# Talking-heads attention with a gated feed-forward: packing the last queries of three images, and another order inside a step

## The chip, the cores and the metric

The kernel runs on one core of a Trainium2 chip. The metric is the device time of one execution in microseconds (us); lower is better. TensorE (PE) multiplies matrices, VectorE (DVE) and ScalarE (ACT) work element by element and empty PSUM, where the products arrive, GpSimd (POOL) works on SBUF, SyncE (SP) mostly issues DMAs. In a profile PEld is the loading of weights into TensorE.

## The reference, cut to what matters

```python
def _attn_ref(q, k, v, w_pre, w_post):        # q, k, v: 4 images, 12 heads, 448 positions, 64
    scores = scale * np.matmul(q, k.transpose(0, 1, 3, 2))
    scores = np.einsum('bhij,hg->bgij', scores, w_pre)        # first mixing, over heads
    scores = scores - np.max(scores, axis=-1, keepdims=True)
    attn = np.exp(scores)
    attn = attn / (np.sum(attn, axis=-1, keepdims=True) + 1e-09)
    attn = np.einsum('bhij,hg->bgij', attn, w_post)           # second mixing
    return np.matmul(attn, v)

# then, with x = the attention's output as 1792 rows of 768:
#   xn = x / rms(x) * rms_g;  out = (silu(xn @ w_gate) * (xn @ w_val)) @ w_out
```

## The kernel before

**Chunks and steps.** An image's 448 query positions are cut into four chunks of 120, 120, 110 and 98 (`CHUNK`, `OFF`, `WIDE`); ten positions of the last one are computed with the third. The 16 chunks are numbered n; n % 4 == 3 is the last chunk of an image. A chunk is worked on in six steps (five in a last chunk), 92 steps t in all (`steps`, line 402), each on two groups u of 2 x 5 positions by all 12 heads.

**What a step does** (the loop at lines 494 to 554). The product of q and k is made well ahead: `qk_mm` (line 134) computes one pair of heads of a later chunk as four 64 x 64 products into two PSUM tiles `qk`, one per head j; `qk_evac` (line 152) copies them out to `st`, j = 0 on ACT (line 162), j = 1 on DVE (line 160), and issues one or two DMAs that scatter `st` to `r`, so that a row of `r` holds one head and one position. `premix` (line 181) multiplies `r` by `wk_pre`, which gives the first mixing `sp` for u = 0 and u = 1. DVE takes the negated row maxima `nm` (`rowmax`, line 196), ACT the exponential `e` with its sums (`expo`, line 203). `norm` (line 206) adds 1e-9 (`t`), takes the reciprocal (`rp`) on DVE and multiplies the second mixing's weights by it on POOL (`wn`, line 215). One step later `postmix` (line 217) multiplies `e` by `wn`, which gives the second mixing `pm`, transposed; `evac_a` (line 241) copies its two halves to `at_all`, on ACT (line 265) and DVE (line 263). `av_mm` (line 274) multiplies `at_all` with v, `av_copy` (line 296) copies the result out to `xt` on ACT, and POOL adds squares for the norm of x (`x_sum`).

**What sets the order.** The order on each engine is the order in which the loop's body is written; a scheduler moves nothing. Within a step the order on TensorE is

```python
                order = sp[:1] + qk[1:] + sp[1:] + qk[:1]     # line 511
```

that is: `sp` for u = 0, `qk` of head j = 1, `sp` for u = 1, `qk` of head j = 0; then `postmix` of the step before, then `av_mm`. The `qk` and `sp` tiles have one buffer per head and per u, so a product into one waits for the copy (or the exponential) that empties it. On DVE a step is: `nm`, `nm`, copy of `st`, copy of `at_all`, `t`, `rp`.

**Work beside it.** From step 23 on the first feed-forward weights are converted from float64 in pieces (`first_w`, line 774): eight rounds of seven steps, five of which have one DVE instruction on `wac` (`to_f32`, line 559). Scales of x, of the weights and of the gains are computed in chains of very small DVE instructions on `stats` and `square` (`chain`, line 443), and `sq_all` (line 349) the norm of x of one image, with four products of TensorE at its stage 0. The chains stand in `last_at`, at the end of a step.

**After step 91** come the feed-forward products, until the end.

The first five `qk` pairs of chunk 1 are made before the loop (`AHEAD`), and from then on one pair is made per step until all are done, at step 84.

## Time and profile before

| | us |
|---|---|
| three runs | 823.37, 830.76, 831.68 (median 830.76) |
| the profiled execution | 822.48 |
| its span, first to last instruction | 820.6 |
| PE busy / DVE busy / ACT busy | 794.4 (97%) / 634.5 (77%) / 507.3 (62%) |
| the 92 steps, from the first `nm` on | 317.75 |

The profile is of one execution. "Busy" counts the time in which an instruction ran; a busy TensorE is not one at its peak. Step t begins here with its first `nm` on DVE (two per step, one in the last step of an image), so that a stretch of the trace can be told by the number of `nm` in it. In rows of instructions the columns are start and duration in us, engine, line, operation, out<-in, and how many were merged; in brackets the engine's idle time before it and what ended it.

### The profile page before, as it was taken

The numbers are of one execution on the slowest core, as the hardware profiler recorded it, in microseconds if no ns is written. First come the engines' busy times: TensorE is split into PE (matmuls) and PEld (weight loads), VectorE is DVE, ScalarE is ACT, GpSimd is POOL, SyncE is SP. The second block draws the span as 40 slices with busy tenths as digits, with TensorE's granted clock in tenths as the row PEclk, the third lists the DMA queues.
The fourth block names the chain that finished last, engine by engine and source line by source line (L and its number), as shares of the span: only waits on it lengthen the run. The fifth ranks groups of instructions, "written<-read, shape, count | busy, mean of one in ns | idle before, by whom it ended". The sixth has DMA issues, their size and how long they took to land.

```text
span 820.6 us, 26914 instructions
## 1 busy us (share of the span) xinstructions
PE 794.4 (97%) x10806; PEld 485.2 (59%) x10806; DVE 634.5 (77%) x1322; ACT 507.3 (62%) x1133; POOL 350.4 (43%) x467
## 2 busy tenths in 40 slices
PE   7899999999999989899999999999999999999998
PEld 2567777767776767655555555555555555555555
DVE  5777878888798867888788978997889676547562
ACT  3677778777776867664344454545444546969850
POOL 7212343454355435843624433426144359452310
PEclk9999999999999999999999999999999999999999
DMA  7777777777876754564255644754546446566641
GB/s 216 208 216 217 219 229 222 228 219 232 222 234 200 211 147 150 158 230 118 66 177 150 183 129 127 216 149 121 174 145 201 133 127 184 157 199 176 184 135 67
DMA packets 81902, 145.15 MB, mean 177 GB/s; under 512 B 10527, under 2 KB 72797, under 8 KB 81779
## 3 DMA queue, kind: packets, MB, share of 16 engines
q1 hardware_dynamic: 79982, 139.83, 57.0%
q0 software_dynamic: 832, 2.06, 1.0%
q8 instruction: 85, 1.39, 0.7%
q10 hardware_dynamic: 965, 1.56, 0.6%
q14 instruction: 38, 0.31, 0.1%
HBM read 72.83 MB, written 31.88 MB: 128 GB/s over the span
## 4 chain that ended last, share of the span: by engine, by line
PE 86%; DMA 8%; DVE 2%; issue 1%; ACT 1%; POOL 1%; SPq 0%; ACTq 0%; DVEq 0%; POOLq 0%
PE qk L140 7%; PE pm L226 7%; PE sp L187 7%; PE av L294 6%; PE pg L750 6%; PE pg L752 6%; PE pv L752 6%; PE pg L751 6%; PE pv L751 6%; PE pv L750 6%; DMA r<-st 6%; PE po L751 6%; PE po L750 6%; PE po L752 6%; DMA wraw<-in_wgv 1%
## 5 line engine op out<-in xcount | busy, mean ns | idle before, releaser
L187 PE MATMUL sp<-r,wk_pre 64*64 64x448 f32 x720 | 167.4, 542 | 5.4 <-DMA r<-st 3.5
L203 ACT ACTIVATE e<-sp,nm 128x448 f32<-128x448 f32 x180 | 114.3, 637 | 84.8 <-DVE nm L196 82.4
L140 PE MATMUL qk<-k,q 64*64 64x448 f32 x768 | 152.6, 559 | 5.9 <-DMA q<-in_q 4.1
L196 DVE TENSOR_REDUCE nm<-sp 128x1 f32<-128x448 f32 x180 | 110.3, 620 | 44.1 <-PE sp L187 27.4
L215 POOL TENSOR_SCALAR wn<-wk,rp 128x60 f32<-128x60 f32 x180 | 59.5, 345 | 181.8 <-DVE rp L212 109.7
L226 PEld LDWEIGHTS pm<-wn,e 60*64 60x64 f32 x5040 | 106.1, 134 | 37.6 <-POOL wn L215 23.8
L226 PE MATMUL pm<-wn,e 60*64 60x60 f32 x5040 | 106.7, 220 | 4.2 <-issue 4.1
L798 POOL TENSOR_TENSOR sg<-sg,u 128x448 f32<-128x448 f32 x36 | 45.9, 1275 | 151.2 <-ACT sg L795 106.7
L294 PE MATMUL av<-at_all,v 64*64 64x240 f32 (+6 forms) x1728 | 93.6, 316 | 4.6 <-issue 2.6
L750 PE MATMUL pv<-x,wh 128*128 128x448 f16 x264 | 93.0, 352 | 0.0
L752 PE MATMUL pv<-x,wl 128*128 128x448 f16 x264 | 93.0, 352 | 0.0
L752 PE MATMUL pg<-x,wl 128*128 128x448 f16 x264 | 93.0, 352 | 0.0
L751 PE MATMUL pv<-x,wh 128*128 128x448 f16 x264 | 93.0, 352 | 0.0
L751 PE MATMUL pg<-x,wh 128*128 128x448 f16 x264 | 93.0, 352 | 0.0
L750 PE MATMUL pg<-x,wh 128*128 128x448 f16 x264 | 93.0, 352 | 0.0
L750 PE MATMUL po<-h,fac 128*128 128x448 f16 (+1 forms) x258 | 89.8, 348 | 0.0
L751 PE MATMUL po<-h,fac 128*128 128x448 f16 (+1 forms) x258 | 89.8, 348 | 0.0
L752 PE MATMUL po<-h,fac 128*128 128x448 f16 (+1 forms) x258 | 89.8, 348 | 0.0
L750 PEld LDWEIGHTS <-wh 128*128 128x128 f16 x528 | 51.7, 98 | 48.2 <-issue 0.2
L751 PEld LDWEIGHTS <-wh 128*128 128x128 f16 x528 | 51.7, 98 | 48.3 <-issue 0.3
L752 PEld LDWEIGHTS <-wl 128*128 128x128 f16 x528 | 51.7, 98 | 48.2
L187 PEld LDWEIGHTS sp<-r,wk_pre 64*64 64x64 f32 x720 | 60.3, 133 | 27.2 <-ACT e L203 13.2
(167 smaller groups left out, 1567.3 us busy)
## 6 DMA issues: line engine op xcount, KB each, us to landing
r<-st SPq DMA_DIRECT2D x117, 210.0 KB
hraw<-td SPq DMA_DIRECT2D x84, 224.0 KB
wraw<-in_wgv SPq DMA_DIRECT2D x20, 768.0 KB
td<-keep SPq DMA_DIRECT2D x48, 224.0 KB
wraw<-in_wo SPq DMA_DIRECT2D x12, 768.0 KB
r<-st SPq DMA_DIRECT2D x44, 157.5 KB
v<-in_v SPq DMA_DIRECT2D x24, 256.0 KB
k<-in_k SPq DMA_DIRECT2D x24, 224.0 KB
```

Of the source, the lines that this page charges most:

```text
L140: nc.tensor.matmul(ps[j][m, :S], qt[n][sl, hp, m], kt[n // NC, hp][sl], start=True, stop=True)
L187: nc.tensor.matmul(o, wk_pre[sl], rt[n][sl, 2 * p + v_], start=True, stop=True)
L196: nc.vector.tensor_reduce(t, ps[:, :S], AX.X, ALU.max, negate=True)
L203: nc.scalar.activation(e, ps[:, :S], AF.Exp, bias=nmx.pop((n, p, u)), accum_out=sm[n, p][:, u : u + 1])
L215: nc.gpsimd.tensor_scalar(wn[n, p][:, u], wk, r[:, u : u + 1], 1.0, ALU.mult, ALU.mult)
L226: nc.tensor.matmul(o[:, :, at_], e_[sl, j : j + JT], w_[sl].rearrange("p (s i) -> p s i", s=2), start=True, stop=True)
L294: nc.tensor.matmul(x, vt[b, hp][sl, j, c_], a, start=(c_ == 0), stop=(c_ == JC - 1))
L750: nc.tensor.matmul(ps, a, xh[:, kk, at_], start=(kk == 0), stop=False)
L751: nc.tensor.matmul(ps, a, xl_[:, kk, at_], start=False, stop=False)
L752: nc.tensor.matmul(ps, a2, xh[:, kk, at_], start=False, stop=(kk == KT - 1))
L798: nc.gpsimd.tensor_tensor(h, sg, u, ALU.mult)
```

## The change

For images two to four (`shared(n)` is true for the last chunk of each) the last chunk no longer has a score tile of 128 columns of q. Of its positions 24 are computed in the eight columns that each of the other three chunks leaves free, and the other 64 as a half tile: `qk_mm` then makes two pairs of heads at once, so that the chunk needs three steps with `qk` instead of six. The scores of positions that travel with another chunk are scattered by additional DMAs (`rest_out`) into a new tile `rest`, from which the first and the last step of that chunk take their first mixing, with a second arrangement of weights in `wk_pre`. The steps with `qk` are no longer one per step in a row: those of chunk n begin one step after chunk n - 2 has begun (`starts`), so four steps in the middle and all from step 80 on have none.

Inside a step `av_mm` now comes ahead of `postmix`, and `norm` ahead of the copies of `at_all` and of POOL's sums. The conversion of weights and the small chains are moved from the ends of a step to the place between `rowmax` and the copy of `st` (`odd_at`), the chains one step later than they stood; `sq_all` and the scales of x begin at other steps. `st` is one tile for twelve heads instead of twelve buffers. The scratch space for descriptors of POOL's DMAs is halved.

```diff
+def shared(n):
+    return n >= NC and n % NC == NC - 1
...
+        def two(j, i):
+            sl, u = slice(64 * j, 64 * j + 64), (i + j) % 2
+            nc.tensor.matmul(ps[i][64 * u : 64 * u + 64, :S], qt[n][sl, 2 * hp + i], kt[n // NC, 2 * hp + i][sl], start=True, stop=True)
+
+        if shared(n):
+            return [[lambda j=j, i=i: two(j, i) for j in (i, 1 - i)] for i in range(2)]
...
+        if j and n >= NC and hp % 3 == 2:
+            rest_out(n, hp // 3, st)
+        if shared(n):
+            for u in range(2):
+                waiting.append((n, 2 * (2 * hp + j) + (u + j) % 2, st[64 * u : 64 * u + 64, at_], 0, SPLIT, False))
+            if at_ < 3 or at_ == 5:
+                for args in waiting:
+                    gather(*args)
+                waiting.clear()
...
+    def rest_out(n, half, st):
+        if shared(n):
+            for i in range(2):
+                for u in range(2):
+                    rows = slice(100 + 12 * u, 112 + 12 * u)
+                    nc.sync.dma_start(rest[rows, slot(n - 3 + i)], st[64 * u + 60 + 2 * i : 64 * u + 62 + 2 * i, :6])
+        else:
+            nc.sync.dma_start(rest[4 + half : 4 + half + 95 : 2, slot(n)], st[120:, 6 * half : 6 * half + 6])
...
+        last = shared(n)
+        kind = int(last and p in (0, PAIRS[-1] - 1))
+
+        def rows(sl, i):
+            if not kind:
+                return rt[n][sl, i - 2 * last]
+            return rest[sl, slot(n - 3 + (i if p == 0 else 2))]
...
-            nc.tensor.matmul(o, wk_pre[sl], rt[n][sl, 2 * p + v_], start=True, stop=True)
+            nc.tensor.matmul(o, wk_pre[sl, kind], rows(sl, 2 * p + v_), start=True, stop=True)
...
-    for i, a in enumerate([(n, hp) for n in range(1, NCHUNK) for hp in range(H // 2)][AHEAD:]):
-        qk_at[i].append(a)
+    odd_at = [[] for _ in range(T + 40)]
+    starts, t_ = {}, -1
+    for n in range(1, NCHUNK):
+        for hp in range(H // 4 if shared(n) else H // 2):
+            if n == 1 and hp < AHEAD:
+                continue
+            t_ = max(t_ + 1, first[n - 2] + 1 if n > 1 else 0)
+            starts.setdefault(n, t_)
+            qk_at[t_].append((n, hp))
...
-                job(first[n] + i, lambda i: first_w(i), i)
+                (odd_at if i % 7 < 5 else jobs_at)[first[n] + i].append((lambda i: first_w(i), i))
...
-        t = first[NC * b + NC + 2] + (5 if b < B - 2 else 3)
-        for i in range(17):
-            last_at[t + max(i - 2, 0) // 3].append((sq_all, b, i))
-        chain(t, lambda b=b: x_scale_ops(b), 2 if b < B - 2 else 4)
+        t = (first[10] - 1, first[13] + 4, first[14] + 3)[b]
+        for i in range(16):
+            last_at[t + (max(i - 1, 0) if i < 4 else 3 + (i - 4) // 3)].append((sq_all, b, i))
+        chain((first[6] + 8, first[10] + 6, first[14] + 3)[b], lambda b=b: x_scale_ops(b), 1 if b < B - 2 else 2)
...
                 rowmax(*back(0))
-                flush()
+                flush(1)
+                for f, *a in odd_at[t]:
+                    f(*a)
                 expo(*back(0))
             if t in (T - 2, T):
                 early(t - T)
+            for a in av_at[t]:
+                av_mm(*a)
             if back(1):
                 postmix(*back(1))
-            for a in av_at[t]:
-                av_mm(*a)
             for a in qk_at[t][:1]:
                 for j in range(2):
                     qk_evac(*a, j)
-            if back(0) and t >= T - 2:
+            if back(0):
                 norm(*back(0))
+            flush()
             if back(1):
                 for v_ in range(2):
                     evac_a(*back(1), v_)
...
+            for x in last_at[t]:
+                f, *a = x
+                if t >= T - 1 or f is sq_all and not a[1]:
+                    f(*a)
+                else:
+                    odd_at[t + 1].append(x)
```

How this moves instructions is seen at three places. First VectorE before, steps 31 and 32, in the second round of the weights' conversion (`nm` are the row maxima, `wac` the conversion's tile):

```order
L565 TENSOR_SCALAR wac<-wac 128x384
L196 TENSOR_REDUCE nm<-sp 128x1 x2
L160 COPY st<-qk 128x448
L263 COPY at_all<-pm 128x84x5
L210 TENSOR_SCALAR t<-s 128x2
L212 RECIPROCAL rp<-t 128x2
L566 TENSOR_SCALAR wac<-wac 128x384
L196 TENSOR_REDUCE nm<-sp 128x1 x2
L160 COPY st<-qk 128x448
L263 COPY at_all<-pm 128x84x5
L210 TENSOR_SCALAR t<-s 128x2
L212 RECIPROCAL rp<-t 128x2
```

and VectorE now, the same two steps:

```order
L241 TENSOR_REDUCE nm<-sp 128x1 x2
L617 TENSOR_SCALAR wac<-wac 128x384
L194 COPY st<-qk 128x448
L255 TENSOR_SCALAR t<-s 128x2
L257 RECIPROCAL rp<-t 128x2
L308 COPY at_all<-pm 128x84x5
L241 TENSOR_REDUCE nm<-sp 128x1 x2
L618 TENSOR_SCALAR wac<-wac 128x384
L194 COPY st<-qk 128x448
L255 TENSOR_SCALAR t<-s 128x2
L257 RECIPROCAL rp<-t 128x2
L308 COPY at_all<-pm 128x84x5
```

The instruction on `wac` stood ahead of a step's maxima and now stands between them and the copy of `st`; `t` and `rp` stood behind the copy of `at_all` and now stand ahead of it.

Second VectorE before, steps 34 and 35:

```order
L568 SCALAR_TENSOR_TENSOR wac<-wraw,wac 128x384
L196 TENSOR_REDUCE nm<-sp 128x1 x2
L160 COPY st<-qk 128x448
L263 COPY at_all<-pm 128x84x5
L210 TENSOR_SCALAR t<-s 128x2
L212 RECIPROCAL rp<-t 128x2
L196 TENSOR_REDUCE nm<-sp 128x1 x2
L160 COPY st<-qk 128x448
L263 COPY at_all<-pm 128x84x5
L210 TENSOR_SCALAR t<-s 128x2
L212 RECIPROCAL rp<-t 128x2
```

and VectorE now, the same two steps:

```order
L241 TENSOR_REDUCE nm<-sp 128x1 x2
L620 SCALAR_TENSOR_TENSOR wac<-wraw,wac 128x384
L255 TENSOR_SCALAR t<-s 128x2
L257 RECIPROCAL rp<-t 128x2
L308 COPY at_all<-pm 128x84x5
L241 TENSOR_REDUCE nm<-sp 128x1 x2
L255 TENSOR_SCALAR t<-s 128x2
L257 RECIPROCAL rp<-t 128x2
L308 COPY at_all<-pm 128x84x5
```

The two copies of `st` are gone from these steps (on ScalarE and TensorE the other copy and the four products), since chunk 7 has three such steps and not six.

Third TensorE, step 31 with the beginning of step 32 (`av` is the product with v, `pm` the second mixing), before:

```order
L187 MATMUL sp<-r_123,wk_pre 64x448 x2
L140 MATMUL qk<-k_0_827,q_2195 64x448 x2
L187 MATMUL sp<-r_123,wk_pre 64x448 x2
L140 MATMUL qk<-k_0_827,q_2195 64x448 x2
L226 MATMUL pm<-wn,e 64x2x30 x28
L294 MATMUL av<-at_all,v_0_1033 64x220 x4
L294 MATMUL av<-at_all,v_0_1033 64x2x55 x4
L187 MATMUL sp<-r_123,wk_pre 64x448 x2
```

and TensorE now, the same stretch:

```order
L232 MATMUL sp<-r_126,wk_pre 64x448 x2
L153 MATMUL qk<-k_1_863,q_2130 64x448 x2
L232 MATMUL sp<-r_126,wk_pre 64x448 x2
L153 MATMUL qk<-k_0_795,q_2130 64x448 x2
L339 MATMUL av<-at_all,v_0_995 64x220 x4
L339 MATMUL av<-at_all,v_0_995 64x2x55 x4
L271 MATMUL pm<-wn,e 64x2x30 x28
L232 MATMUL sp<-r_126,wk_pre 64x448 x2
```

The order of `sp` and `qk` is as it was; `av` has gone from behind `pm` to ahead of it. The numbers in these rows count buffers; the second operand of `qk` is now a tile that two pairs of heads share.

## Rows read from the trace of the kernel before

**Rows 1.** Stretches, `nm` (line 196) alone: stretch, length, DVE busy (x number), PEclk, DMA, GB/s

```profile
40.62:58.88 18.26, 7.37 (x13) 1.00 0.73 221
117.78:133.32 15.54, 6.22 (x10) 1.00 0.78 234
133.32:140.60 7.28, 2.49 (x5) 1.00 0.83 233
154.03:159.22 5.19, 1.25 (x2) 1.00 0.78 234
210.92:219.34 8.42, 2.46 (x5) 1.00 0.82 223
232.82:237.30 4.48, 1.25 (x3) 1.00 0.86 270
289.66:312.96 23.30, 6.14 (x11) 1.00 0.49 139
76.71:289.66 212.95, 75.59 (x123) 1.00 0.76 221
```

**Rows 2.** Order of time, steps 8 and 9, all engines

```profile
48.37 0.61 DVE L160 COPY st<-qk 128x448 f32<-128x448 f32 x1
...
49.10 0.22 PEld L140 LDWEIGHTS qk<-k,q 64*64 64x64 f32 x4 [0.50 <-PE pm L226]
...
50.28 0.57 PE L187 MATMUL sp<-r,wk_pre 64*64 64x448 f32 x2
...
50.89 0.62 DVE L196 TENSOR_REDUCE nm<-sp 128x1 f32<-128x448 f32 x1 [0.54 <-PE sp L187]
```

**Rows 3.** Order of time, steps 17 and 79: copy of `st` and weights of the next `qk`

```profile
78.11 0.61 DVE L160 COPY st<-qk 128x448 f32<-128x448 f32 x1
...
78.80 0.13 PEld L140 LDWEIGHTS qk<-k,q 64*64 64x64 f32 x1
...
287.49 0.62 DVE L160 COPY st<-qk 128x448 f32<-128x448 f32 x1
...
288.22 0.22 PEld L140 LDWEIGHTS qk<-k,q 64*64 64x64 f32 x4
```

**Rows 4.** Pieces of the chain of waits in step 30

```profile
121.61 0.79 PE pm L226 x47
...
122.52 0.75 PE av L294 x15
```

**Rows 5.** Order of time, VectorE, step 51

```profile
190.89 0.34 DVE L564 TENSOR_SCALAR wac<-wraw 128x384 int32<-128x384 int32 x1
...
192.03 0.62 DVE L196 TENSOR_REDUCE nm<-sp 128x1 f32<-128x448 f32 x1 [0.27 <-PE sp L187]
```

**Rows 6.** Stretch of steps 17 to 79, `wac` alone: DVE busy (x), ACT busy (x), PEclk, DMA

```profile
76.71:289.66 212.95, 17.35 (x40) 4.94 (x16) 1.00 0.76 221
```

**Rows 7.** The same stretch, `stats` alone

```profile
76.71:289.66 212.95, 8.21 (x48) 0.00 (x0) 1.00 0.76 221
```

**Rows 8.** Who waited for whom, steps 17 to 79: us in total, times, longest

```profile
PEld pm L226 <- POOL wn L215: 16.7, 47, 0.8
...
PE pm L226 <- issue: 3.0, 4, 1.1
```

**Rows 9.** Order of time, a step without `qk`: step 86

```profile
318.23 0.97 PE L187 MATMUL sp<-r,wk_pre 64*64 64x448 f32 x8
```

**Rows 10.** Groups of ScalarE, steps 17 to 79: busy us, mean ns, idle before

```profile
L265 ACT ACTIVATE at_all<-pm 128x420 f32<-128x420 f32 (+1 forms) x66 | 35.8, 548 | 0.4 <-PE pm L226 0.4
...
L304 ACT ACTIVATE xt<-av 128x480 f32<-128x480 f32 x16 | 8.2, 577 | 0.0
```

**Rows 11.** Order of time, POOL and VectorE, around the first `wac`

```profile
96.42 0.69 POOL L332 TENSOR_TENSOR xt<-xt 128x240 f32<-128x240 f32 x1
96.54 0.79 DVE L564 TENSOR_SCALAR wac<-wraw 128x384 int32<-128x384 int32 x1 [0.18 <-DMA wraw<-in_wgv]
```

**Rows 12.** Order of time, SyncE's issues, step 8

```profile
47.56 1.59 SPq L179 DMA_DIRECT2D r<-st  x2
```

More of the change, by code (lines that the diff above doesn't have):

```diff
@@ L150, in alone, with gather @@
         in_turn(*parts)
+    def gather(n, h, src, lo, hi, held_):
+        w, at_ = RH * (hi - lo), 2 * RH * lo
+        if h < H - 1:
+            parts = [(h, 2 * RH, at_, 2 * w)]
+        else:
+            parts = [(h, RH, at_, w), (64, RH, at_ + w, w)]
+        for row, k_, from_, many in parts:
+            dst = rt[n][row : row + (k_ - 1) * GAP + 1 : GAP, lo:hi]
+            x = src[from_ : from_ + many]
+            if held_:
+                held.append((dst, x))
+            else:
+                turn = h if row < H else h + 1
+                if n:
+                    eng = nc.gpsimd if n == 1 and 6 <= h < 2 * AHEAD else nc.sync
+                else:
+                    eng = nc.sync if turn % 2 else nc.gpsimd if turn < 6 else nc.scalar
+                eng.dma_start(dst, x)
@@ L163, in qk_evac @@
[L163 to L179 removed]
+        at_ = 2 * hp + j
@@ L248, in evac_a @@
             n_, a = n + 1, 40
-        elif c < NC - 1:
-            n_, a = n, RH * t
+        elif not shared(n):
+            n_, a = n, RH * t if t < 8 else 45 if c == NC - 1 else RH * t
         else:
-            n_, a = n, 45 if p == PAIRS[-1] - 1 else RH * t
+            n_, a = n, 45 if p == PAIRS[-1] - 1 else 30 + RH * t if p == 0 else RH * (t - 2)
         lo, hi = SLOTS[n_]
@@ L362, in rsqrt @@
         if eng is nc.vector:
-            bits = var
             step = [
@@ L369, in rsqrt @@
         else:
-            bits, i = spare, spare.bitcast(I32)
             step = [
@@ L427, in attention_moe @@
             for i in range(2):
-                job(6 * n - 16 + 3 * i, load_q, n, 3 * i, 3, nc.sync)
+                job(starts[n] - 5 + (1 if shared(n) else 3) * i, load_q, n, 3 * i, 3, nc.sync)
         for hp in range(H // 2):
@@ L439, in attention_moe @@
             if n % NC == NC - 1 and n + 1 < NCHUNK:
-                job(t + 1, load_k, n // NC + 1, hp)
+                for i in (2 * hp, 2 * hp + 1) if shared(n) else (hp,):
+                    job(t + 1, load_k, n // NC + 1, i)
     chains = []
@@ L536, in part_a @@
                     evac_a(*back(1), v_)
-            if back(0) and first[NCHUNK - 1] <= t < T - 2:
-                norm(*back(0))
             for op in sum_ops[: 1 if t < first[NCHUNK - 2] else 2 if t <= T else 4]:
@@ L541, in part_a @@
                 sum_ops.pop(0)
-            if back(0) and t < first[NCHUNK - 1]:
-                norm(*back(0))
-            for a in qk_at[t][1:]:
-                alone(qk_mm(*a))
-                for j in range(2):
-                    qk_evac(*a, j)
-            for f, *a in last_at[t]:
-                f(*a)
+            if t in (3, 7):
+                nc.gpsimd.memset(rest[:, t // 2 - 1 : t // 2 + 1], 0.0)
+            for x in last_at[t]:
+                f, *a = x
+                if t >= T - 1 or f is sq_all and not a[1]:
+                    f(*a)
+                else:
+                    odd_at[t + 1].append(x)
             for a in done:
@@ L692, in attention_moe, with flush @@
     lows, defer = [], []
-    def flush():
-        while lows:
-            lows.pop(0)()
+    def flush(many=2):
+        for op in lows[:many]:
+            op()
+        del lows[:many]
     def x_split(b, kk, eng):
```

137 lines of the change are left out of this document (74 added, 63 removed).

## The prediction

> **What bounds the kernel now.** I read the profile by stages, then one step, then the waits. The reader is to see first that the time falls in two parts. The 92 steps take 317.75 us (the small table of the times); after them come the feed-forward products, which the change doesn't touch, so all that follows is about the steps. A table of stretches by the number of `nm` [rows 1] gives the length of a step: steps 6 to 11, without any product with v, take 18.26 / 6 = 3.04 us, and steps 29 to 33, with that product and with a `wac` instruction in each, 15.54 / 5 = 3.11 us. The average of steps 17 to 79 is 212.95 / 63 = 3.38 us, so about a tenth of that stretch lies in disturbed steps: 40 (5.19 us) and 63 (4.48 us), where `sq_all` and a chain of small instructions meet, 57 and 58 (8.42 us), 34 and 35 (7.28 us). Steps 80 to 84 take 23.30 us, 4.66 each.
>
> Second, what sets 3.04 us where nothing disturbs. Follow one turn in order of time [rows 2]. The copy of `st` on VectorE ends at 48.37 + 0.61 = 48.98; the weights of the next `qk` of head j = 1 are loaded at 49.10; `sp` of u = 1, which stands behind it on TensorE, ends at 50.28 + 0.57 = 50.85; its maximum `nm` starts at 50.89, and behind that comes the next copy of `st`. The gap from the end of that copy to the next `sp` end is 1.87 us, `nm` 0.62 and the copy 0.61 less some overlap give the rest: a ring of 3.05 us through both engines, closed by the single buffer of `qk`. I looked in each of steps 17 to 79 whether the weights of `qk` are loaded within 0.15 us of the end of the copy: in 42 of the 63 they are, the first and the last of them after 0.08 and 0.11 us [rows 3]. In the other 21 something else was later.
>
> Third, TensorE is nearly as tight. In step 30 the chain of waits is TensorE alone, `pm` with 0.79 us at 121.61 and `av` with 0.75 us at 122.52 [rows 4], so ring and TensorE both stand at 3.05 to 3.1 us. What VectorE does ahead of `nm` is covered: in step 51 the `wac` instruction runs at 190.89, and still VectorE then waits 0.27 us for `sp` before the second maximum [rows 5].
>
> **The change part by part.** The sum is made against the profiled execution, 822.48 us, which lies 1% below the median of the three runs, 830.76, and near the lowest, 823.37.
>
> 1. *Odd work inside the ring.* `wac` instructions and the small chains now stand between `nm` and the copy of `st`, that is inside the ring, where before they lay in VectorE's wait for `sp`. There are 40 `wac` instructions with 17.35 us [rows 6], 0.434 us each; 38 of them fall in steps that have `qk`. Neighbours on VectorE overlap by about 0.08 us (in rows 2 the next instruction could start before 48.98), so 38 x 0.35 = 13.4 us. Of small instructions I count 55 in steps with `qk` from 17 to 78; on `stats` one takes 8.21 / 48 = 0.17 us [rows 7], less overlap 0.12, so 6.6 us, and 0.9 more for two of them that reduce 448 columns. Together 20.9 us. Above: all of it counts. Below: nothing, if TensorE is later in each of these steps. I take the part of steps in which the ring was last, 42/63: +13.9 us.
>
> 2. *Steps without qk in the middle.* Steps 34, 35, 57 and 58 took 7.28 + 8.42 = 15.7 us [rows 1]. They lose four products and two copies each, and the ring with them. What is left on TensorE is `sp` 0.97 [rows 9], `pm` 0.79 and `av` 0.75 [rows 4], 2.5 us; on ScalarE two exponentials, a copy of `at_all` and, in some, copies of `xt`. I take 2.7 us each plus 1.8 us for stalls of TensorE without a releaser, of which single ones reach 1.1 us [rows 8] and which I see no reason to lose: 12.6 us, so -3.1 us. Between -5 and 0.
>
> 3. *The lumps of steps 40 and 63.* `sq_all` and the scales go elsewhere, one or two small instructions per step. The two steps took 9.67 us [rows 1], and 2 x 3.4 stays, the rest being counted in item 1; TensorE still does the products of `sq_all`, in step 57 beside free time and once in step 79. -2.4 us.
>
> 4. *The tail.* Steps 80 to 84 have no `qk` any more. Steps 80 and 81 at 2.7 us, 82 and 83 with twice the products with v at 3.1, step 84 with `sq_all` at 4.0, and 1.7 us of the same stalls: 17.3 instead of 23.30 [rows 1], -6.0 us. Between -8 and -2.
>
> 5. *av ahead of pm, norm ahead of the copies.* `pm` waited for `wn` 47 times and 16.7 us in all [rows 8], but it is the weight load that waits; the products of `qk` ahead of it still run, as the unbroken chain of rows 4 shows. Once `av` covers the wait, the ring is last. I take -1.0 us, between -4 and 0.
>
> 6. *Copies of xt in front of the exponentials.* `pm` now ends a step, so ScalarE's copy of `at_all` (0.55 us) can end later, and the two copies of `xt` (0.58 us each, more where they are split) behind it, and then the exponential [rows 10]. `norm`, which waits for the exponential, stands ahead of `at_all` on VectorE and so ahead of the next `nm`. There are some 22 such steps; a step with odd work has room for the delay. +0.1 us each, +2.0 us; between 0 and 22 x 0.55 = 12.
>
> 7. *The rest.* Waits of `sp` for the scatter DMAs end, since the last chunks' rows are made earlier: -0.6 us. One more small instruction in the setup: +0.2 us. The DMAs of `rest_out` are 30 more, issued by SP at 0.8 us each [rows 12], and in a shared chunk's third step eleven issues come together, some 9 us; the tile `st` that they read is written again four steps, about 11 us, later. I cost this at nothing; without that cover it would be up to 3 us at each of two places.
>
> Sum: 13.9 - 3.1 - 2.4 - 6.0 - 1.0 + 2.0 - 0.6 + 0.2 = +3.0 us, so 825.5 us by the profiled execution and 833.8 us by the median. Since it is open which of the two levels a measurement shows, I predict the middle, 829.5 us.
>
> One rule is weighed here against item 1. In the trace the first `wac` instruction took 0.79 us instead of 0.34, while POOL's addition of 0.69 us, begun before it, was running [rows 11]. The Trainium skill ("SBUF — State Buffer", section "SBUF: two separate sides") says that VectorE and GpSimd share one pair of ports as an exclusive lock, for some kinds of VectorE instruction, and that the later one waits until the other has ended. Rows 11 look like that. By the rule the price of item 1 would rise wherever POOL's sums run at that moment; by the row it is 0.45 us for one instruction, and if all 38 met a sum, 17 us. I leave it out of the sum, because POOL's sums follow `wn`, which comes earlier now, and end about when the maxima do.
>
> **The rivals.**
>
> *TensorE is the clock (faster).* If in steps with `av` TensorE is always as late as the ring, odd work falls into its shadow and item 1 is near 2 us instead of 13.9. For it: rows 4, and steps 29 to 33 are as long as those without odd work. Against it: rows 3, and the 42 of 63. Then the sum is -8.9 us: 817.6 us on the same middle level, 826.5 us without a change. With items 2 and 4 at their best it is 1.5% faster.
>
> *The ring is the only clock (slower).* Each step with `qk` costs 3.05 us and its odd work in full: item 1 is 20.9 and, where the exponential is late as well, item 6 up to 5. The place is VectorE between the second `nm` and the copy of `st`; it decides as soon as the wait of `qk` for that copy is last in nearly all steps and not in two thirds. For it: once odd work is inside, TensorE has 0.35 us to spare, so nothing else can be last. Against it: disturbed steps, where part of it is hidden. Sum +13.0: 839.5 us, 1.6% slower. The lock of rows 11 would add to this case.
>
> *The saving does not arrive.* Half tiles save three steps of `qk` per image, but if the exponentials' ring through the buffers of `sp` holds 3.1 us also without `qk`, items 2 and 4 shrink to about -5 together: +7 us, 833.5 us, still within 1%.
>
> **How the numbers follow.** Forecast, with the third rival in it: 0.45. TensorE the clock: 0.30. The ring alone: 0.25. About 1%, 8.3 us, is what a measurement of this kernel can tell from no change. Of the forecast nearly all lies within 1%; of the first rival 0.27 falls beyond 1% faster, and 0.02 comes from the forecast's own edge; of the second 0.24 beyond 1% slower, with 0.03 from the edge. So faster 0.29, within 1% 0.44, slower 0.27. The forecast's own range is 820 to 838 us. The range for 8 in 10 goes from the first rival at the lower level, some 812, to the second at the upper, some 845.
>
> **What would show it right or wrong.** Item 1: in the changed profile the copy of `st` follows the `wac` instruction, the weights of `qk` load within 0.15 us of its end in nearly all odd steps, and these steps are 3.3 to 3.5 us long, while steps without odd work stay at 3.05. It is wrong if odd steps stay at 3.1. Items 2 and 4: steps 34, 35, 57, 58, 80 and 81 at about 2.7 us; wrong at 3.1. Item 5: the wait of `pm` for `wn` all but gone, without a gain in steps 6 to 11. Item 6: steps with copies of `xt` longer than their neighbours. The forecast as a whole is wrong if the stretch of steps 17 to 79 gets shorter than 205 us or longer than 225.

## The result, and the profile after

The changed kernel takes 833.81 us (median of 18 runs, 831.62 to 839.15), the kernel before 827.88 us in the 18 runs beside it (820.71 to 831.68). The ratio is 1.0095, with a 95% interval from 1.0066 to 1.0124: slower by nearly 1%. The forecast was +3.0 us; measured are 5.9 us between the medians and 7.9 by the ratio (0.0095 x 827.9).

The profiled executions stand further apart, 822.48 and 833.87 us. That of before lies 5.4 us below its median, that of after at its median; so of the 11.4 us between the traces about half belongs to the choice of execution. Where a step of the argument hangs on a few microseconds, the ratios below decide, not two traces. That the forecast's sum also names 833.8 us is chance: it was counted from 830.76, the median of three runs, where 18 runs have 827.88.

The ratios leave out executions more than 1.5% above the fastest of the same kernel; beside the first four runs of the next section one execution of 816.05 us takes five of 17 of the kernel before out in this way, and over all executions the ratios of (a), (b) and (c) would be 0.3% lower, that of all three 0.1%.

The stretches of after, `nm` alone, answer to [rows 1]. The columns: stretch, length, VectorE and ScalarE busy (x number), granted clock, DMA share, GB/s.

```profile
75.86:300.27 224.41, 75.95 (x124) 88.61 (x246) 1.00 0.73 214
136.17:142.03 5.86, 2.29 (x5) 2.68 (x8) 1.00 0.89 278
157.60:160.74 3.14, 1.25 (x2) 1.45 (x4) 1.00 0.82 261
218.27:224.79 6.52, 2.30 (x5) 2.68 (x8) 1.00 0.76 220
240.43:243.85 3.42, 1.23 (x2) 1.45 (x4) 1.00 0.94 261
300.27:320.05 19.78, 5.75 (x11) 6.70 (x20) 0.96 0.34 97
320.05:346.72 26.67, 6.92 (x12) 8.05 (x24) 0.90 0.43 125
```

In order: steps 17 to 79; 34 and 35; 40; 57 and 58; 63; 80 to 84; 85 to 90. The last stretch took this long before:

```profile
312.96:335.87 22.91, 6.93 (x13) 8.06 (x24) 0.93 0.44 129
```

Three things are to be read here. Steps 17 to 79 became 11.5 us longer, although the four steps without `qk` and the two lumps became shorter. Steps 80 to 84 became 3.5 us shorter, and steps 85 to 90, which the forecast did not speak of, 3.8 us longer: the tail as a whole gained nothing. And in the tail TensorE's granted clock is 0.96 and 0.90, where it was 1.00 [rows 1] and 0.93.

A step with odd work (step 25, order of time; answers to [rows 2, 5]):

```profile
105.04 0.62 DVE L241 TENSOR_REDUCE nm<-sp 128x1 f32<-128x448 f32 x1 [0.46 <-PE sp L232]
...
105.59 0.35 DVE L618 TENSOR_SCALAR wac<-wac 128x384 int32<-128x384 int32 x1
...
105.85 0.62 DVE L194 COPY st<-qk 128x448 f32<-128x448 f32 x1
...
106.58 0.22 PEld L149 LDWEIGHTS qk<-k,q 64*64 64x64 f32 x4 [0.21 <-PE pm L271]
...
107.37 0.61 DVE L241 TENSOR_REDUCE nm<-sp 128x1 f32<-128x448 f32 x1
```

`wac` now stands between `nm` and the copy of `st`, and the weights of `qk` are loaded 0.11 us after that copy ends (105.85 + 0.62 = 106.47; the row puts the wait down to `pm`, but `pm` had ended at 106.40, before the copy). So it is, within 0.15 us, in 45 of the 58 steps with `qk` from 17 to 79, against 42 of 63 before. Steps 24 to 27 take 13.69 / 4 = 3.42 us.

Who waited for whom (us in total, times, longest): steps 17 to 79 on TensorE's weight load and on VectorE (answers to [rows 8]).

```profile
PEld av L339 <- ACT xt L353: 4.3, 12, 0.7
...
PEld av L339 <- ACT xt L349: 3.0, 10, 0.6
```

```profile
DVE nm L241 <- PE sp L232: 20.8, 45, 1.0
DVE t L255 <- ACT e L248: 5.9, 17, 0.9
...
DVE st L194 <- DMA rest<-st: 3.2, 2, 2.1
```

The whole run before, and after:

```profile
PEld pm L226 <- POOL wn L215: 23.8, 65, 1.1
...
PEld av L294 <- ACT xt L304: 0.4, 1, 0.4
```

```profile
PEld av L339 <- ACT xt L349: 10.0, 18, 1.9
...
PEld av L339 <- ACT xt L353: 5.1, 13, 0.8
...
PEld pm L271 <- POOL wn L260: 2.3, 10, 0.3
```

In the whole run `pm` waited 23.8 us for `wn` before and waits 2.3 now, as forecast. In its place `av` waits 15.1 us for ScalarE's copies of `xt`, where before it waited 0.4. Half of that lies in the tail. There one step, 84, took 7.11 us:

```profile
315.95 0.60 POOL L260 TENSOR_SCALAR wn<-wk,rp 128x60 f32<-128x60 f32 x2
316.51 0.56 POOL L377 TENSOR_TENSOR xt<-xt 128x210 f32<-128x210 f32 x1
317.15 0.63 POOL L378 TENSOR_TENSOR sum<-sum,xt 128x210 f32<-128x210 f32 x1
```

```profile
317.83 0.55 PE L392 MATMUL pss<-ones,sum 128*112 128x1 f32 x4 [1.16 <-POOL sum L378]
318.32 1.72 PE L232 MATMUL sp<-r,wk_pre 64*64 64x448 f32 x8
319.79 2.62 PE L339 MATMUL av<-at_all,v 64*64 64x240 f32 x32
```

The column sums of `sq_all` (`pss`) stand ahead of the next `sp` on TensorE and need POOL's last sum, which now comes behind `wn`. TensorE stood still for 1.16 us, and the granted clock by single microseconds (after length and busy times of the five engines) shows what followed:

```profile
317.00:318.00 1.00, 0.17 (x2) 0.17 (x2) 0.00 (x0) 0.00 (x0) 0.87 (x3) 1.00 0.00 0
...
319.00:320.00 1.00, 1.00 (x12) 0.48 (x8) 0.00 (x0) 0.00 (x0) 0.00 (x0) 0.50 0.00 0
320.00:321.00 1.00, 1.00 (x16) 0.60 (x13) 0.95 (x2) 0.23 (x1) 0.00 (x0) 0.50 0.00 0
...
322.00:323.00 1.00, 1.00 (x67) 0.97 (x60) 0.33 (x2) 0.11 (x2) 0.32 (x2) 1.00 0.00 0
```

From about 318.4 to 321.8 us the clock is at the lower level, 1.2 of 2.4 GHz, and the eight products of `sp` take 1.72 us instead of 0.97 [rows 9]. Not every standstill does this. In step 89 TensorE stood still for 1.15 us, from 335.04 to 336.19, until a copy of `xt` was done, and the clock stayed at 1.00 (columns as above):

```profile
334.00:336.00 2.00, 1.04 (x23) 0.26 (x16) 1.53 (x3) 1.69 (x4) 1.83 (x6) 1.00 1.02 285
336.00:338.00 2.00, 1.81 (x90) 1.76 (x94) 1.33 (x6) 1.61 (x6) 1.27 (x4) 1.00 0.37 101
```

The second fall of the clock in this tail, at 342.3 us, follows a standstill of 1.82 us ahead of feed-forward products; the kernel before has one like it, 1.87 us, with the clock falling at 332.8.

### The profile page after: what moved, and what is told of

Same layout as the page of the kernel before. It is cut to its first block, busy times and chain, and to the rows that moved or that the text cites. A ratio compares the mean times of both kernels' runs of the same rounds, so it can differ in the third digit from the quotient of the medians.

```text
span 832.0 us, 26745 instructions
## 1 busy us (share of the span) xinstructions
PE 810.2 (97%) x10734; PEld 496.6 (60%) x10734; DVE 629.9 (76%) x1311; ACT 506.5 (61%) x1124; POOL 347.5 (42%) x469
## 3 DMA queue, kind: packets, MB, share of 16 engines
q10 hardware_dynamic: 965, 1.56, 0.6%
## 4 chain that ended last, share of the span: by engine, by line
PE 92%; DVE 2%; DMA 2%; ACT 1%; issue 1%; POOL 1%; SPq 1%; ACTq 0%; DVEq 0%; POOLq 0%
PE sp L232 10%; PE pm L271 9%; PE qk L149 8%; PE av L339 7%; PE pg L803 6%; PE pv L804 6%; PE pg L805 6%; PE pv L805 6%; PE pg L804 6%; PE pv L803 6%; PE po L804 6%; PE po L803 6%; PE po L805 6%; PE qk L153 1%; DVE nm L241 1%
## 5 line engine op out<-in xcount | busy, mean ns | idle before, releaser
L232 PE MATMUL sp<-r,wk_pre 64*64 64x448 f32 x684 | 162.3, 549 | 1.2 <-ACT e L248 0.7
L241 DVE TENSOR_REDUCE nm<-sp 128x1 f32<-128x448 f32 x180 | 110.3, 620 | 40.0 <-PE sp L232 27.6
L260 POOL TENSOR_SCALAR wn<-wk,rp 128x60 f32<-128x60 f32 x180 | 54.7, 319 | 195.9 <-DVE rp L257 159.0
L271 PE MATMUL pm<-wn,e 60*64 60x60 f32 x5040 | 122.7, 222 | 2.3 <-issue 2.3
L271 PEld LDWEIGHTS pm<-wn,e 60*64 60x64 f32 x5040 | 115.9, 135 | 7.2 <-issue 2.5
L339 PE MATMUL av<-at_all,v 64*64 64x240 f32 (+6 forms) x1728 | 114.7, 319 | 2.1 <-ACT xt L349 1.9
L149 PE MATMUL qk<-k,q 64*64 64x448 f32 x624 | 106.6, 564 | 8.0 <-DMA q<-in_q 4.0
L339 PEld LDWEIGHTS av<-at_all,v 64*64 64x64 f32 x1728 | 91.0, 135 | 32.7 <-ACT xt L349 10.0
```

The source lines that it names most:

```text
L149: nc.tensor.matmul(ps[j][m, :S], qt[n][sl, hp, m], kt[n // NC, hp][sl], start=True, stop=True)
L232: nc.tensor.matmul(o, wk_pre[sl, kind], rows(sl, 2 * p + v_), start=True, stop=True)
L241: nc.vector.tensor_reduce(t, ps[:, :S], AX.X, ALU.max, negate=True)
L260: nc.gpsimd.tensor_scalar(wn[n, p][:, u], wk, r[:, u : u + 1], 1.0, ALU.mult, ALU.mult)
L271: nc.tensor.matmul(o[:, :, at_], e_[sl, j : j + JT], w_[sl].rearrange("p (s i) -> p s i", s=2), start=True, stop=True)
L339: nc.tensor.matmul(x, vt[b, hp][sl, j, c_], a, start=(c_ == 0), stop=(c_ == JC - 1))
```

## The experiments

Ratios are to the kernel before, run beside each, with 95% intervals. 1% is 8.3 us.

**The three orders, one by one.** Four edits of the changed kernel; the other kernels of this group are made of them. In all of them the rest of the change stays: the half tiles, the one tile `st`, the halved scratch space, and the other places in time of `sq_all` and the scales. So "half tiles alone" below means the change without its three orders.

```diff
 # (a) odd work ahead of nm
+                for f, *a in odd_at[t]:
+                    f(*a)
                 rowmax(*back(0))
                 flush(1)
-                for f, *a in odd_at[t]:
-                    f(*a)
 # (b) av behind pm: postmix(*back(1)) ahead of the loop over av_at[t]
 # (c) norm behind evac_a and the sums (from the last chunk on behind evac_a,
 #     in the last two steps where it stands), as in the kernel before
```

(a), (b), (c) and all three:

> The changed kernel with the odd work (wac and the small chains) ahead of the first nm of its step, outside the ring; all else as changed. Ring theory (odd work between nm and the copy of st is on the path in two thirds of the steps): 8 to 14 us faster than the changed kernel, so 820 to 826 us where the changed one has 833.8; steps 24 to 27 fall from 3.4 to 3.1 us each. Rival, TensorE is the clock: within 2 us of the changed kernel and the same step lengths. Rival, the copies of xt: within 4 us, the steps with odd work and without xt fall by less than 0.1 us.

> The changed kernel with the product with v behind the second mixing again. By the prediction (term 5) this loses 1 us: 834.8 us. Theory of the copies (ahead of pm, av waits on TensorE for ScalarE's copies of xt, 10.0 + 5.1 us of waits in the changed profile against 0.4 before): those waits fall below 1 us, pm waits for wn again (2.3 us now, 23.8 before), and the tail of steps 80 to 91 gets 4 to 7 us shorter than its 49.45 us; the whole 5 to 10 us faster than the changed kernel, 824 to 829 us.

> The changed kernel with reciprocals and weights (rp, wn) behind the copies and sums again. By the prediction nothing rests on this alone: within 2 us of the changed kernel, 832 to 836 us. Theory that the early norm holds up the copies of at_all on VectorE (norm waits for the exponential): 3 to 6 us faster, with fewer waits of sp and av for the copies. Rival, early weights are what keeps pm from waiting: pm's wait for wn rises from 2.3 to over 10 us and the time by 3 to 8 us.

> All three orders as in the kernel before, the half tiles alone. By the prediction's terms 2, 3, 4 and 7: 11.9 us faster than the kernel before, ratio 0.986. Theory that the new orders cost and the half tiles gain: ratio 0.985 to 0.992, steps 80 to 84 at 17 to 19 us. Rival, the half tiles' own gain is given back elsewhere (rest_out on SP, the later odd work, POOL's sums): ratio 0.997 to 1.003.

Then (b) with (c), (a) with (b), and (a) with (c), which leave one new order each:

> Half tiles and the odd work between nm and the copy of st; the product with v and the weights stand as before. The prediction's ring (term 1 alone, +13.9, bounds 0 to 20.9) against the run with all orders as before, 831.0 us: 841 to 847 us and steps 24 to 27 at 3.4 us where that run has 2.85 to 3.1. Rival, VectorE is one chain and it does not matter where the odd work stands: within 3 us of 831.0.

> Half tiles and rp and wn ahead of the copies and sums; odd work and the product with v stand as before. Theory of VectorE's second ring (nm, exponential, t, copy of at_all, nm: t waits for ScalarE's exponential 60 times and 25.7 us where odd work is ahead of nm, 6 times and 1.05 us where the weights are late): t waits over 20 us and the time is 838 to 844 us, 7 to 13 above the run with all orders as before. Rival, the 842.4 us came from the product with v ahead of pm: within 3 us of 831.0.

> Half tiles and the product with v ahead of the second mixing; odd work and weights stand as before. Theory of the copies of xt (av waits on TensorE for them): 1 to 4 us above the run with all orders as before, 832 to 835 us, with over 8 us of waits of av for xt. The prediction's term 5 (-1.0, -4 to 0): 827 to 831 us.

Measured:

| odd work in the ring | weights early | av ahead of pm | median us | ratio |
|---|---|---|---|---|
| | | | 831.04 | 1.0067 [1.0024, 1.0111] |
| x | | | 835.50 | 1.0110 [1.0075, 1.0145] |
| | x | | 837.58 | 1.0127 [1.0087, 1.0167] |
| | | x | 832.69 | 1.0077 [1.0050, 1.0104] |
| x | x | | 834.81 | 1.0133 [1.0081, 1.0184] |
| x | | x | 837.98 | 1.0170 [1.0118, 1.0221] |
| | x | x | 842.39 | 1.0225 [1.0166, 1.0284] |
| x | x | x (the change) | 833.81 | 1.0095 [1.0066, 1.0124] |

Every expectation of a gain from undoing one order fell. Undoing (a) alone, where 8 to 14 us less were expected, made it 8.6 us slower (842.39). The trace of that run shows why, in VectorE's waits from step 17 to 79:

```profile
DVE t L255 <- ACT e L248: 25.7, 60, 0.9
DVE nm L241 <- PE sp L232: 5.2, 10, 1.1
...
DVE st L194 <- DMA r<-st: 1.5, 1, 1.5
```

With the weights early, `t` stands ahead of the copy of `at_all` and of the next `nm`, and VectorE waits there for the exponential, in 60 steps. Odd work placed behind `nm` runs in that wait; placed ahead of `nm` it is added to it. With the weights late, `t` waited for the exponential twice in this stretch (0.6 us). So early weights close a second ring (`nm`, exponential, `t`, copy of `at_all`, `nm`), and with the odd work moved into its gap, as in the change, `t` waits 5.9 us. Early weights alone cost 0.6% against half tiles alone (0.8% by the medians), and (in the profile of that run) `t` waited 27.3 us, as expected. With the odd work in the gap they cost nothing that can be told: 834.81 us for the pair, 835.50 for odd work alone. (In the traces the pair took 219.33 us for steps 17 to 79 and odd work alone 226.20, but the first trace is of the fastest of its six executions, 829.92 us.) The product with v ahead costs 0.1% alone (0.2% by the medians), inside the intervals, with 19.7 us of waits for `xt`; undoing it in the changed kernel took these waits away (0.4 us), left the time unchanged (834.81 against 833.81) and brought `pm`'s wait for `wn` back (12.2 us). It is an exchange of two waits. Undoing the early weights (c) cost 4.2 us, the price of the rival named there, but not by its wait: `pm` waited 3.1 us for `wn`, since `av` ahead of it covers that. Odd work in the ring alone cost 4.5 us where the ring theory wanted 10 to 16.

What matters most is the first line. Half tiles with all orders as before were to gain 11.9 us; they are 0.67% slower than the kernel before.

**SP's backlog.** In that run the engines waited 12.5 us for DMAs from step 13 on, 8.0 of them with copies of `st` and 4.0 with `wac`. Two edits: the scatters of heads 3 and 4 of a shared chunk go out at once, and then `rest_out` goes to POOL.

```diff
-            if at_ < 3 or at_ == 5:
-                for args in waiting:
-                    gather(*args)
-                waiting.clear()
+            for args in waiting:
+                gather(*args)
+            waiting.clear()
```

```diff
-                    nc.sync.dma_start(rest[rows, ...], st[...])
+                    behind.append((rest[rows, ...], st[...]))
...
+            for args in behind[:2]:      # at the end of a step, after the sums
+                nc.gpsimd.dma_start(*args)
+            del behind[:2]
```

The first edit, with half tiles alone and with the changed kernel:

> Half tiles alone (all three orders as before), and the scatters of heads 3 and 4 of a shared chunk issued as soon as their copy is made, not together with rest_out and the scatter of head 5 in one burst. Theory that SP's burst eats the half tiles' gain (in the run with the orders as before, VectorE and ScalarE waited some 12 us for DMAs: 8.5 us of copies of st for r and rest, 4.0 us of wac for wraw): those waits fall below 5 us and the time by 4 to 8 us, to 823 to 827 us where that run had 831.0. Rival, SP is loaded all along and the wait moves elsewhere: within 2 us of 831.0.

> The changed kernel with the same spread of the scatters and nothing else. Waits of st for DMAs are 4.7 us there (2.06 at 145.9, 1.11 at 227.9, 0.53, and ScalarE's beside them); theory: they go and the time falls by 2 to 4 us, to 830 to 832 us. Rival: steps 36 and 59 are long for another reason (twice the products with v), no change within 1 us.

Measured: 832.03 us (1.0055 [1.0029, 1.0080]) and 841.65 us (1.0172 [1.0132, 1.0211]). The changed kernel became 7.8 us slower by an edit that only sends two heads' scatters earlier. The trace of the first one, SP in order of time, and VectorE's copies around it:

```profile
137.03 1.31 SPq L184 DMA_DIRECT2D r<-st  x1
138.39 0.48 SPq L828 DMA_DIRECT2D wraw<-in_wgv  x1
138.97 0.84 SPq L116 DMA_DIRECT2D k<-in_k  x2
140.07 1.58 SPq L184 DMA_DIRECT2D r<-st  x2
141.75 2.73 SPq L214 DMA_DIRECT2D rest<-st  x4
144.52 2.48 SPq L184 DMA_DIRECT2D r<-st  x3
```

```profile
131.77 0.62 DVE L194 COPY st<-qk 128x448 f32<-128x448 f32 x1
...
146.43 0.62 DVE L194 COPY st<-qk 128x448 f32<-128x448 f32 x1 [4.95 <-DMA rest<-st]
```

The last copy of the chunk ended at 132.4, and SP came to `rest_out` at 141.75, 9.4 us late, behind scatters and loads that it issues one at a time. The next chunk's first copy overwrites what `rest_out` reads and waits 4.95 us. Sending the scatters first had only put `rest_out` further back: with half tiles alone it came 4.7 us after the last copy. Both edits together, with half tiles alone, with the changed kernel, and with odd work in the ring as the only new order:

> Half tiles alone with the scatters spread, and the four DMAs rest_out of a shared chunk issued by POOL, two at the end of each of two steps, not by SP. In the run with SP they were issued some 9 us after the last copy of st, behind 10 scatters and loads, and the next chunk's first copy waited 4.95 and 4.84 us for them; steps 36 to 39 and 59 to 62 took 20.0 us each. Theory that SP's backlog ahead of rest_out is the price of the half tiles: those waits fall below 0.5 us, steps 36 to 39 and 59 to 62 to 13 to 14 us, the time by 10 to 16 us, to 816 to 822 us, 0.6 to 1.3% faster than the kernel before. Rival, the scatters to r are late as well and take the place of rest_out: 827 to 831 us. Rival, POOL's 0.57 us per DMA hold up wn: pm's wait for wn grows by over 4 us.

> The changed kernel with the same two edits (scatters spread, rest_out of shared chunks on POOL). Theory of SP's backlog: against the run with the spread alone (841.65 us; waits of 5.44 and 5.20 us) 12 to 16 us faster, 826 to 830 us, so 4 to 8 below the changed kernel. What is then left against the half tiles alone with the same edits is the price of the three orders: 5 to 10 us by the step tables.

> The half tiles with both edits of the DMAs and the odd work between nm and the copy of st, the other two orders as before: the price of the odd work inside the ring where no DMA wait hides it. Ring theory (term 1, two thirds of the steps): 10 to 14 us above the run with odd work ahead of nm and the same DMA edits. From the pair without these edits (835.5 against 831.0): 4 to 5 us above. Rival, no price: within 2 us.

Measured: 826.22 us (0.9987 [0.9957, 1.0016]), 835.99 us (1.0100 [1.0070, 1.0130]) and 834.61 us (1.0087 [1.0050, 1.0123]). Steps 36 to 39 and 59 to 62 in the run with the first edit and then with both:

```profile
139.10:159.10 20.00, 4.99 (x8) 5.75 (x16) 0.91 0.69 212
...
223.69:243.74 20.05, 4.85 (x8) 5.70 (x16) 0.83 0.69 203
```

```profile
142.07:157.56 15.49, 5.00 (x9) 5.80 (x16) 1.00 0.79 245
...
222.46:235.52 13.06, 4.75 (x8) 5.54 (x16) 1.00 0.73 219
```

The wait falls from 4.95 and 4.84 us to 1.56 and none, and the granted clock stays at 1.00, where TensorE's standing still had lowered it. The backlog was worth 5.8 us of the time, below the expectation (10 to 16 us); against half tiles alone, without the first edit, both edits gain 4.8. The Trainium skill ("DMA: Bandwidth & Descriptors", section "Issuing engines are not separate DMA queues") says that issuing from several engines saves only the sequencer's time to start a DMA, usually small beside the DMA. What was saved in this run is such time; that it is small does not hold for SP here, where twelve issues, six scatters of 0.7 to 1.3 us and six loads of 0.3 to 0.5, made up the 9 us with the gaps between them. In the changed kernel the same two edits bring nothing (1.0100 against 1.0095): VectorE's waits for `rest_out` go from 3.2 us to 2.4. That its longer steps gave SP the time already is likely, but no run shows it.

Odd work in the ring costs 1.00% here (0.9987 to 1.0087), 8.3 us, and this time the intervals lie apart. Early weights with the product ahead cost another 0.13%, inside the intervals.

**Odd work in the ring of the kernel before.** The loops of (a) reversed, in the kernel before, without half tiles (cut; `wac` and the small chains are put into `odd_at` as in the change):

```diff
                 rowmax(*back(0))
                 flush()
+                for f, *a in odd_at[t]:
+                    f(*a)
```

> The kernel before with wac and the small chains between nm and the copy of st, nothing else changed: term 1 alone. Prediction: +13.9 us (0 to 20.9), ratio 1.017. From the half-tile pair: +8.4 us, ratio 1.010. Theory that longer steps also take away stalls of TensorE (instruction packets): stalls without a releaser fall from 6.4 to 2 to 4 us, which is the difference between the two numbers.

Measured: 848.11 us, 1.0250 [1.0199, 1.0300], so 20.7 us: as much as the upper bound of term 1 and the rival "the ring is the only clock". The stretch of steps 17 to 79 with `nm`, and with `wac` alone:

```profile
76.34:316.94 240.60, 76.37 (x124) 89.33 (x246) 0.98 0.66 197
```

```profile
76.34:316.94 240.60, 21.12 (x40) 4.91 (x16) 0.98 0.66 197
```

Steps 24 to 27 take 13.82 us, 1.6 more than before (12.22), 0.4 each, as a ring that pays in full would have it. But the agreement of 20.7 with 20.9 is in good part chance. Of the 27.6 us by which this stretch is longer in the two traces, 9.0 lie in two steps, 41 and 64 (7.70 and 7.23 us, before 2.75 and 3.14): there the first small instructions of `sq_all` and of the scales meet in the ring, and TensorE waited 2.0 and 1.5 us for them, where the change begins the two at different steps. `wac` itself took 21.12 us instead of 17.35 [rows 6]. And TensorE's stalls without a releaser did not fall from 6.4 us, as expected, but rose to 10.4.

**Where the half tiles' own gain goes.** Half tiles for the last image alone, with the three orders as before and both edits of the DMAs (cut to the line that decides); then the changed kernel with the old places of the weights and of the product with v from step 80 on:

```diff
 def shared(n):
-    return n >= NC and n % NC == NC - 1
+    return n == B * NC - 1
```

> Half tiles for the last image only (last chunk), the three orders as before, scatters spread and rest_out on POOL. Steps 17 to 78 are then those of the kernel before but for the places of sq_all and the scales. Theory (the half tiles' gain arrives in the tail, 5.3 us there, and is lost in the middle): 4 to 6 us faster than the kernel before, ratio 0.993 to 0.995, steps 80 to 84 at 17 to 18 us. Rival, TensorE's stalls without a releaser give it back as they did in the middle: ratio 0.998 to 1.002.

> The changed kernel, with the product with v and the weights in the order of before from step 80 on only. Theory (term 4's 6 us arrived and the new orders gave them back in the tail: 49.45 us for steps 80 to 91 after, 44.0 with the old orders): the tail falls to 44 to 45 us, the whole by 4 to 6 us, 828 to 830 us, ratio 1.002 to 1.004. Rival, the tail is bound by POOL's sums: within 2 us of the changed kernel.

Measured: 831.96 us, 1.0046 [1.0009, 1.0084], where a gain was expected; and 831.77 us, 1.0066 [1.0033, 1.0099]. The second shows the tail, steps 80 to 84 and 85 to 90:

```profile
301.36:319.48 18.12, 5.75 (x10) 6.71 (x20) 1.00 0.39 110
319.48:344.33 24.85, 6.91 (x13) 8.05 (x24) 0.94 0.42 120
```

Together 42.97 us instead of 46.45: in the trace the old orders give back more than half of the 6 us in the tail. The time is 0.3% less, which the intervals do not tell from nothing. With half tiles alone these stretches took 17.55 and 23.49. The rest is not in one place. In the first run steps 80 to 84 took 19.90 us, 3.4 less than before, and steps 17 to 79 219.78, 6.8 more than before, 6.2 of it ahead of its first half tile in step 78 (its trace is of a middling execution, that of before of a fast one). What this run shares with all the others is the rest of the change (one tile `st`, the places of `sq_all` and the scales, the scratch space); no run here takes that out.

In the trace of the fastest half-tile version (the one of 826.22 us; its trace is of its fastest execution, 820.87) TensorE often stands still with no releaser, as here in step 22, while the DMA view of 93.9 to 95.4 us has one packet of the instruction queue:

```profile
94.34 1.16 PE L270 MATMUL pm<-wn,e 60*64 60x60 f32 x51
96.71 0.27 PE L270 MATMUL pm<-wn,e 60*64 60x60 f32 x2 [1.21 <-issue]
```

```profile
q8 instruction: 1, 0.02, 5.6%
```

That packet, 16 KB, started at 93.98 and took 1.34 us; TensorE goes on 1.4 us after its end. Over the steps from 55 us on, such stalls of over 0.3 us sum to 6.4 us in the kernel before, 13.0 in this version and 2.3 after the change; of 119 of them up to step 91 in all 20 traces of this case, 113 end between 1.2 and 1.75 us after such a packet. To see whether DMA traffic delays the packets, the scatters of later ordinary chunks were cut to half their columns (the sums of those score tiles are then made with older rows), in the half-tile version, in the kernel before and in the changed kernel:

```diff
-            ... ((0, H if n % NC < NC - 1 else WHOLE),)
+            ... ((0, (H if n < 4 else H // 2) if n % NC < NC - 1 else WHOLE),)
```

> The fastest half-tile version with the scatters to r of all ordinary chunks from the fifth on at half their columns (the other half of r keeps older rows): as many DMAs, about a third less traffic in the middle. Theory that TensorE's stalls without a releaser are instruction packets delayed by DMA traffic: 13.0 us of them in that version fall below 5 us, steps 17 to 79 from 215 to 205 to 209 us and the time by 5 to 10 us. Rival, the packets are asked for late whatever the traffic: stalls stay at 9 us or more and the time falls by less than 3 us.

> The kernel before with the scatters to r of all ordinary chunks from the fifth on at half their columns (the other half of r keeps older rows). If traffic is what eats the half tiles' gain, the kernel before gains less from lighter scatters than the half tiles did (9 us): 0 to 3 us, ratio 0.996 to 1.000. If both pay it: 7 to 10 us, ratio 0.988 to 0.992, and the half tiles' own gain is then not lost to traffic.

> The changed kernel with the same lighter scatters. Theory that its steps of 3.4 us are set by VectorE's rings and not by traffic: 0 to 4 us below 833.8 (the waits of st for DMAs, 4 us, may go), ratio 1.005 to 1.010. If traffic sets it: 7 to 10 us below, ratio 0.997 to 1.001.

Measured: 817.22 us (0.9888 [0.9836, 0.9939]), 819.81 us (0.9902 [0.9868, 0.9935]) and 829.20 us (1.0035 [1.0005, 1.0066]). The DMA share in the middle fell from 0.73 to 0.60 in the half-tile version, the stalls only from 13.0 to 10.0 us, so by its stalls that run spoke for the rival and by its time for the theory. The kernel before gains as much as the half tiles do, 1.0%, and the changed one 0.6%. So traffic is a price that the kernel before pays too, and the half tiles' gain is not lost to it. In the changed kernel the engines' waits for DMAs fell from 6.0 us to none, which would be enough for its 0.6%; in the kernel before they were 2.8 us of the 8 gained.

## Why the prediction was wrong, step by step

The sign was right and the order inside a step was read rightly; the sum came out too low by 3 to 5 us, mostly at its fourth term. In the two traces steps 17 to 79 became 11.5 us longer, where the terms for them add up to some 9; the tail became 0.2 us longer, where -6.0 was forecast.

1. *Odd work inside the ring* (+13.9). The mechanism holds: the copy of `st` follows `wac`, `qk` loads 0.07 to 0.12 us behind it, odd steps take 3.4 us. The size, two thirds of 20.9, is neither confirmed nor replaced by one number. Moved alone into the kernel before, the odd work costs 20.7 us, a good part of it in two lumps that the change does not have. Beside half tiles it shows as 8.3 us, and as 3.6 (4.5 by the medians), not clear of nothing, where SP's waits are (1.0067 to 1.0110). In these pairs other waits went as the steps became longer: DMA waits from 12.5 to 2.8 us in the one with SP's waits, stalls without releaser from 13.0 to 3.7 in the other. The price of a term depended on what else was late.
2. *Steps without qk* (-3.1): 5.86 + 6.52 - 15.70 = -3.3 us. Right in sum, but by two errors that cancel: single steps took 2.93 us, step 57 with the products of `sq_all` 3.57, not 2.7, and the 1.8 us of stalls that were to stay did not come.
3. *The lumps of steps 40 and 63* (-2.4): 3.14 + 3.42 - 9.67 = -3.1 us. Right.
4. *The tail* (-6.0). This is the step that failed. Steps 80 to 84 gave 3.5 us and steps 85 to 90 took 3.8 more. Steps 80 to 83 took 12.67 us, 0.6 less than forecast with all the stalls; step 84 was put at 4.0 and took 7.11. The forecast counted the four products that fall away and 1.7 us of stalls, and left the tail's own order out: without `qk` nothing lies between `sp` and `av` to cover a copy, so `av` ahead of `pm` waits for `xt` (7.0 us for L349 from step 80 on, in steps 84 to 90), `wn` ahead of POOL's sums makes `pss` wait, and that standstill lowers TensorE's clock. With half tiles and the old orders steps 80 to 84 took 17.55 us, nearly the 17.3 of the forecast; with the old places of `wn` and `av` in the tail of the changed kernel these waits are gone and 3.5 us come back in the trace.
5. *av ahead of pm* (-1.0): the wait for `wn` went, as forecast, and a wait for `xt` of 15.1 us came. In the middle it costs nothing that can be measured; the sign was wrong in the tail, as far as the trace of the run with the old order there shows it.
6. *Copies of xt* (+2.0): the delay was seen, but at the exponential; it is `av` that waits for these copies. The 27 steps from 17 to 79 with such copies took 3.61 us in the mean, the other 36 took 3.53: the 0.1 us each that was forecast.
7. *rest_out at nothing*: the cover named there, four steps, was not enough. The first copies of the next chunks wait 3.2 us in the changed kernel, 2.1 and 1.1 us at the two places where up to 3 us each was written beside it, and 5 us each when `rest_out` is put further back.

Steps 17 to 79 came out at 224.41 us, at the edge of the 205 to 225 that was to hold. Of the rivals, the first, TensorE as the clock, falls: odd steps did not stay at 3.1 us. The second, the ring alone, has its number in the run on the kernel before, but only with the lumps of two steps, and the whole change did not come near its +13.0. The third, +7 us, comes nearest in number, but not by its reason: steps 34, 35, 58, 80 and 81 took 2.93 or 2.94 us, between its 3.1 and the forecast's 2.7, and item 2 kept its saving.

The rule weighed against term 1, the lock between VectorE and GpSimd of the Trainium skill ("SBUF — State Buffer", section "SBUF: two separate sides"), cost nothing in the changed kernel: `wac` took 17.56 us in steps 17 to 79 where it took 17.35 [rows 6]. In the runs where odd work met POOL's sums, with (a) undone and in the kernel before, `wac` took 20.20 and 21.12 us; one instruction there, begun while POOL's addition ran, took 1.46 us and ended 0.4 us behind it. That agrees with the rule, and leaving it out of the sum was right.

What stays open is half of the result on half tiles: step by step they gain 5.3 us in steps 80 to 84 and 3.4 in two lumps, and yet their fastest version is as fast as the kernel before, no faster. Its stalls at instruction packets, 6.6 us more in one trace each, are of that size; no run here takes them away alone, so that is argued and not shown. The other candidate, untested, is the rest of the change: with half tiles for the last image alone the kernel is slower than the kernel before (1.0046) and, if anything, slower than with half tiles for three images (0.9987), so the half tiles themselves may pay and something that comes with them may cost. No version found is faster than the kernel before with its whole work.

## What to carry to other kernels

An instruction that moves on an in-order engine moves from one wait into another: before pricing it, name the ring it leaves and the ring it enters, and who stands in the gap that it fills. When three orders change at once, undoing one of them says little (here undoing (a) or (c) gave a slower kernel than all three or none), so test them from the old side too. And work that falls away is only a gain if what was hidden behind it, an issue queue, a copy, a sum, is not the next to be late.

## What the runs showed of the hardware

TensorE's granted clock fell to its lower level right after one standstill of 1.16 us (from 318.4 to 321.8 us in the changed kernel), stayed up after another of 1.15 us in the same tail, and a wait of 5 us for a DMA brought a stretch of 20 us down to a mean of 0.91 in one place and of 0.83 in another; so a wait can cost more than its own length. TensorE's stalls without a releaser nearly all (113 of 119) end 1.2 to 1.75 us after a 16 KB packet of the instruction queue. And about a fifth less DMA traffic (a share of 0.60 instead of 0.73) made the half-tile version, whose waits named a DMA for only 2.2 us, 1.0% faster, and the kernel before as much.
